# Shorter, more numerous unread products at the start, and the first local scores moved one step forward

## The chip, the cores and the metric

The kernel runs on one core of a Trainium2 chip. The metric is the device time of one execution in microseconds. Five runs of the kernel before the change gave 306.91, 307.11, 307.74, 307.89 and 309.62 us; the median is 307.74. The profile was taken of the run of 307.89 us. Its span, from the first to the last recorded work, is 306.1 us, so 1.8 us of the run lie around the span.

In this text PE is TensorE, DVE is VectorE, ACT is ScalarE, POOL is GpSimd and SP is SyncE. "PE weight load" is the instruction that puts the stationary operand in place ahead of a matmul.

## The reference

Attention with a sparse mask on 8 batches of 8 heads, 576 positions and 64 columns, followed by a two-layer MLP on the 4,608 tokens with a Mish activation:

```
pos = np.arange(S); rel = pos[:, None] - pos[None, :]
mask_local   = (rel >= 0) & (rel < 32)                                   # heads 0 to 3
mask_strided = (rel >= 0) & (pos[None, :] % 32 == pos[:, None] % 32)     # heads 4 to 7
scores = np.where(mask, q @ k.T / sqrt(64), -1e9)
attn   = softmax(scores)
x      = (attn @ v) as [tokens, 512]
h      = x @ w_in                       # 512 -> 2048
out    = (h * tanh(softplus(h))) @ w_out   # 2048 -> 512
```

## The kernel before

The attention of one batch is cut so that only the blocks that the masks leave are computed. A local head (kind "l") has 6 windows of 96 queries against 128 keys. A strided head (kind "s") is taken apart by position modulo 8: for each of 8 residues, 72 queries meet 72 keys. `PARTS` groups the score blocks of a batch into three parts for each kind, one accumulator (two PSUM banks, `acc(i)`, i from 0 to 2) for each part. So `("l", 0)` is the first local part: five (window, head pair) units, with two matmuls of 96 columns for each.

For batch 0 the mask is not multiplied in later. It is put under the scores: `Attn.bias` writes a large negative bias with two matmuls of a unit matrix against a constant (line 297), and `Attn.qk` adds the scores to it in the same accumulator (line 324), then lets ACT take the exponential (line 338). `Attn.pv2` multiplies two blocks of probabilities with v (lines 366 and 371: for strided blocks of batch 0 the values and the row sums come from two matmuls, of 64 columns and of one column), and DVE divides by the row sums (lines 396 and 397), which also frees the accumulator. `t_step` and `t_step_loc0` transpose q and k on PE (lines 237 and 253); DVE or ACT copies the result out of PSUM (lines 179 and 181). `xt` transposes the attention output for the MLP (lines 410 and 420).

The whole program is one order written out by hand (`manual_schedule`): the instructions stand on each engine in the order in which the Python code issues them, and semaphores make one engine wait for another. No planner moves them. Before the loop over the token blocks, batch 0 goes through alone. In order: memsets on DVE and the first loads; the unread products (`fill`, line 547: matmuls of a zeroed tile whose result nobody reads); transposes of strided k and q, with biases and more unread products between them; strided scores; then pairs of strided products `pv2("s", 0)`, `("s", 2)`, `("s", 4)`, `("s", 6)`, with the transposes of local k and q between the first three; local biases and scores; `xt` for the strided half; two unread products; the last local bias and scores; the local products `pv2("l", ...)`. Then begins the first block of the MLP (line 575 is the first layer, line 599 the second), and from there the loop runs 9 blocks of 512 tokens, with the attention of later batches placed between the matmul groups.

The accumulators in this stretch: pair ("s", 0) uses accumulator 0, pair ("s", 2) uses 1, pair ("s", 4) uses 2, pair ("s", 6) uses 0 again, local part 0 uses 1, local part 1 uses 2 and local part 2 uses 0.

Of the kernel before, what the change touches and what calls it, by code (L numbers as in the profile page):

```python
# [40 lines left out]
def kernel(ctx, tc, q, k, v, moe_w_in, moe_w_out, out):  # L41
# [34 lines left out]
    kTs = [const.tile([128, 16 * SU + 48], BF16, name=f"kTs{i}") for i in range(2)]  # L76
# [13 lines left out]
    def acc(i, name):  # L90

        return ps_a.tile([128, 2, 512], F32, tag=f"acc{i}", name=name)

    def tile_t(name):
        return ps_t.tile([128, 512], F32, tag="pt", name=name)
# [81 lines left out]
    def cast(eng, out_, in_):  # L177
        if eng is nc.scalar:
            nc.scalar.copy(out_, in_)  # L179
        else:  # L180
            eng.tensor_copy(out_, in_)  # L181
# [66 lines left out]
    def t_step_loc0(src, dst, hp, eng):  # L248

        tr = tile_t("tr")[:].bitcast(BF16)  # L250
        for j in range(CL):
            for e in range(2):
                nc.tensor.transpose(  # L253
                    tr[64 * e:64 * e + 64, PL * j:PL * j + PL], src[0:PL, 2 * hp + e, j, :],
                    ident[0:PL, 0:PL],
                )
        cast(
            eng, dst.rearrange("c (p j) -> c p j", j=CL),
            tr[:, 0:S].rearrange("c (j p) -> c p j", j=CL),
        )  # L260
# [280 lines left out]
        ]  # L541


    def fill(t, n):

        for _ in range(n):
            nc.tensor.matmul(
                t[:, 0:512], lhsT=kTs[1][:, 512:640], rhs=kTs[1][:, 0:512], start=True, stop=True
            )

    def fill_acc(i, n):
        fill(acc(i, "fill")[:, 0, :], n)

    def segs(t):
        a, e, o, r = 512 * t, 512 * t + 512, 0, []
# [80 lines left out]
    with tc.manual_schedule():  # L636
# [38 lines left out]
        cast(Dv, ks[0][0:PN, 0:2, :], k32[0:PN])  # L675

        a = Attn(0)
        fill_acc(2, 11)
        for hp in range(2):
            t_step(0, "k", hp, Sc if hp else Dv)  # L680
        a.bias("s", 0, 0)
        fill_acc(2, 3)
        for hp in range(2):
            t_step(0, "q", hp, Sc if hp else Dv)
        a.bias("s", 1, 1)
        fill_acc(2, 1)
        a.bias("s", 2, 2)
        for i in range(3):
            a.qk([("s", i)], i)
        fill(tile_t("fill"), 2)  # L690
        a.pv2("s", 0, 0)
        t_step_loc0(kl0, kTl[:, 0, 32:32 + S], 0, Sc)
        t_step_loc0(kl0, kTl[:, 1, 32:32 + S], 1, Sc)
        a.pv2("s", 2, 1)
        t_step_loc0(ql0, qTl[:, 0, :], 0, Sc)
        t_step_loc0(ql0, qTl[:, 1, :], 1, Sc)
        a.pv2("s", 4, 2)
        a.pv2("s", 6, 0)
        for i in range(2):
            a.bias("l", i, i + 1)  # L700
            a.qk([("l", i)], i + 1)
        for hp in range(2):
            rows_v_loc01(0, hp, Dv)
        load_v_loc_h(1)
# [126 lines left out]
```

## Time and profile before

| What | Value |
|---|---|
| median of 5 runs | 307.74 us (306.91 to 309.62) |
| the profiled run, and its span | 307.89 us, 306.1 us |
| PE busy | 298.6 us, 98% of the span |
| DVE, ACT, POOL busy | 155.2, 181.7, 105.2 us |
| mean granted clock of PE | 0.994 of full |
| first unread product (line 547) starts | 1.26 us |
| first strided product (line 366) starts | 10.58 us |
| first local bias (line 297, 480 columns) starts | 14.46 us |
| first local product (line 366, 65 columns) starts | 19.12 us |
| first MLP product (line 575) starts | 20.67 us |

The span is counted from its own start, and the times of the table are on that clock. Busy time of PE includes the depth of its pipeline, so matmuls overlap in it; the distance from one start to the next is the better measure of what a matmul takes. The granted clock is the share of full speed at which PE was allowed to run. A wait is shown behind the instruction that waited, with the instruction that released it. The wait names are inferred: where an instruction waits for several others, the one that came last is shown.

### The profile page before, as it was taken

To read this page: it belongs to the slowest core of one execution; us is meant where nothing else is said; L and a number is where in the kernel's file an instruction comes from. 1 tells how busy PE (TensorE), PEld (TensorE's weight loads), DVE (VectorE), ACT (ScalarE), POOL (GpSimd) and SP (SyncE) were. 2 spreads that over 40 slices of the span, in tenths; PEclk is the share of its full clock that TensorE was granted. 3 is DMA by queue.
4 is the path that set the end of the run, shared out by engine and by line. 5 is a ranking of instruction groups with operands and counts; after the bars stand their busy time and mean duration, and the time that the engine had idled before them with its cause. 6 is when DMAs were issued, how large, how long until landed. Compare 5 with 4: busy or idle time off the path is not lost.

```text
span 306.1 us, 5961 instructions
## 1 busy us (share of the span) xinstructions
PE 298.6 (98%) x2471; PEld 156.5 (51%) x2471; DVE 155.2 (51%) x375; ACT 181.7 (59%) x193; POOL 105.2 (34%) x119
## 2 busy tenths in 40 slices
PE   7999999999999999999999999999999999999995
PEld 3655555544554455444579654445444544444444
DVE  4463266301850077479877888787879850000000
ACT  2666635667446764767866786687668746216501
POOL 8752339860480246004950288029600000000000
PEclk9989999999999999999999999999999999999999
DMA  8999999999999999999759996896730120011011
GB/s 135 171 204 202 198 174 138 148 172 247 166 205 175 199 185 188 109 208 192 111 134 169 192 164 160 184 188 113 111 105 2 42 95 2 0 69 69 2 68 69
DMA packets 97550, 41.81 MB, mean 137 GB/s; under 512 B 79604, under 2 KB 91460, under 8 KB 97524
## 3 DMA queue, kind: packets, MB, share of 16 engines
q1 hardware_dynamic: 71708, 28.84, 52.4%
q0 software_dynamic: 25504, 12.31, 34.0%
q8 instruction: 19, 0.31, 0.5%
q10 hardware_dynamic: 312, 0.28, 0.3%
q14 instruction: 7, 0.06, 0.1%
HBM read 36.82 MB, written 9.44 MB: 151 GB/s over the span
## 4 chain that ended last, share of the span: by engine, by line
PE 91%; DVE 3%; DMA 2%; POOL 1%; issue 1%; ACT 1%; ACTq 0%; POOLq 0%
PE psh L575 41%; PE pso L599 34%; PE pso L626 5%; PE po L366 5%; PE ps L324 4%; DMA lq<-in_q_dram 2%; DVE x_l L383 1%; PE trx L410 1%; DVE x_s L383 1%; PE ps L297 1%; PE tr L253 1%; PE trx L420 1%; DVE rden L382 1%; ACT Ps L338 0%; DVE Pl L346 0%
## 5 line engine op out<-in xcount | busy, mean ns | idle before, releaser
L575 PE MATMUL psh<-xT,w_in 128*128 128x512 bf16 (+3 forms) x648 | 130.6, 355 | 0.7 <-DVE rden L396 0.5
L599 PE MATMUL pso<-w_out,gT 128*128 128x512 bf16 x512 | 121.7, 379 | 0.0
L581 ACT ACTIVATE gT<-psh 128x1024 bf16<-128x1024 f32 x72 | 72.5, 1024 | 46.1 <-PE psh L575 46.1
L575 PEld LDWEIGHTS <-w_in 128*128 128x128 bf16 x648 | 60.8, 98 | 55.3 <-issue 1.1
L599 PEld LDWEIGHTS <-gT 128*128 128x128 bf16 x512 | 45.4, 98 | 46.1
L445 DVE STREAM_TRANSPOSE xs_t<-x_s 32x512 bf16<-32x512 bf16 x48 | 33.7, 702 | 0.9
L606 ACT COPY osb<-pso 128x1024 f32<-128x1024 f32 x16 | 17.6, 1099 | 24.8 <-PE pso L599 14.4
L181 POOL CAST kl<-kl 96x768 bf16<-96x768 f32 x10 | 8.0, 822 | 69.7 <-DMA kl<-in_k_dram 69.7
L382 DVE RECIPROCAL rden<-po 72x4 f32<-72x4 f32 (+1 forms) x98 | 17.3, 177 | 28.7 <-PE po L366 28.5
L436 DVE STREAM_TRANSPOSE xT<-x_l 32x384 bf16<-32x384 bf16 x48 | 27.3, 569 | 0.7
L181 DVE COPY osb<-pso 128x512 f32<-128x512 f32 (+1 forms) x2 | 1.1, 558 | 51.3 <-PE pso L626 51.3
L346 DVE TENSOR_TENSOR Ps<-Ps,consts_sb 72x864 bf16<-72x864 bf16 (+3 forms) x12 | 6.6, 551 | 40.0 <-ACT Ps L338 40.0
L383 DVE TENSOR_TENSOR x_s<-po,rden 72x256 bf16<-72x256 f32 x56 | 23.5, 420 | 1.9
L338 ACT ACTIVATE Ps<-ps 72x864 bf16<-72x864 f32 (+3 forms) x21 | 17.4, 861 | 11.1 <-PE ps L324 11.0
L366 PEld LDWEIGHTS <-Ps 72*128 72x128 bf16 x256 | 15.6, 97 | 11.6 <-DVE Ps L346 0.8
L452 ACT COPY xT<-xs_t 128x576 bf16<-128x576 bf16 x8 | 21.4, 2937 | 0.0
L338 ACT ACTIVATE Pl<-ps 128x960 bf16<-128x960 f32 (+1 forms) x20 | 17.3, 876 | 4.0 <-PE ps L324 4.0
L383 DVE TENSOR_TENSOR x_l<-po,rden 96x256 bf16<-96x256 f32 x42 | 17.7, 421 | 1.4
L366 PE MATMUL po<-vs,Ps 72*128 72x65 bf16 (+1 forms) x256 | 18.2, 194 | 0.1
L179 ACT COPY xT<-trx 128x576 bf16<-128x576 bf16 x15 | 9.6, 639 | 13.0 <-PE trx L420 9.2
L181 POOL CAST vl<-vl 128x768 bf16<-128x768 f32 (+2 forms) x20 | 15.5, 774 | 3.2 <-PE po L366 2.0
L346 POOL TENSOR_TENSOR Ps<-Ps,consts_sb 72x1008 bf16<-72x1008 bf16 (+1 forms) x9 | 14.5, 1639 | 0.8 <-DVE x_l L383 0.7
(93 smaller groups left out, 239.7 us busy)
## 6 DMA issues: line engine op xcount, KB each, us to landing
out_dram<-osb SPq DMA_DIRECT2D x16, 512.0 KB, 4.0
kl<-in_k_dram SPq DMA_DIRECT2D x5, 576.0 KB, 7.2
ql<-in_q_dram SPq DMA_DIRECT2D x5, 576.0 KB, 11.6
vs<-in_v_dram SPq DMA_DIRECT2D x5, 576.0 KB
vl<-in_v_dram SPq DMA_DIRECT2D x5, 576.0 KB, 9.1
w_out<-in_moe_w_out_dram POOLq DMA_DIRECT2D x4, 512.0 KB, 16.6
ks<-in_k_dram POOLq DMA_DIRECT2D x7, 288.0 KB, 8.3
qs<-in_q_dram POOLq DMA_DIRECT2D x7, 288.0 KB, 8.1
```

Source lines behind the costliest of these rows:

```text
L181: eng.tensor_copy(out_, in_)
L338: nc.scalar.activation(pt[0:n, :, 0:nw], t[0:n, :, o0:o0 + nw], AF.Exp, scale=scale)
L346: meng.tensor_tensor(out=pm, in0=pm, in1=mk[0:n, :].unsqueeze(1).unsqueeze(1).to_broadcast([n, 2, nu, w]), op=ALU.mult,)
L366: nc.tensor.matmul(po[:, h, 0:rhs.shape[-1]], lhsT=pt[0:n, c0:c0 + 128], rhs=rhs, start=True, stop=True,)
L382: nc.vector.reciprocal(rden[0:m, :], po[0:m, :, D])
L383: nc.vector.tensor_tensor(out=dst.rearrange("p (h d) -> p h d", h=4), in0=po[0:m, :, 0:D], in1=rden[0:m, :].unsqueeze(2).to_broadcast([m, ...
L436: nc.vector.transpose(dst[32 * q:32 * q + 32, :, :, m:m + 32], src[m:m + 32, :, :, q, :])
L445: nc.vector.transpose(xs_t[32 * q:32 * q + 32, :, :, m:m + 32], src[m:m + 32, :, :, q, :])
L452: nc.scalar.copy(xT[:, 2 + c, t0:t0 + S].rearrange("p (n j) -> p j n", j=CS), xs_t[:, :, c, 0:PN])
L575: nc.tensor.matmul(ps[:, u, o:o + n], lhsT=w_in[:, cc, fc * 128:(fc + 1) * 128], rhs=xT[:, cc, a:a + n], start=(cc == 2 and o == 0), stop= ...
L581: nc.scalar.activation(gT[:, 2 * g:2 * g + 2, :], ps[:], AF.Mish)
L599: nc.tensor.matmul(p[:, ot % 2, :], lhsT=gT[:, fc, 128 * ot:128 * ot + 128], rhs=w_out[:, fc, :], start=(fc == 0), stop=(fc == 15),)
```

## The change

Two edits. The 11 unread products of 512 columns ahead of the strided transposes become 44 of 128 columns; the three other places with unread products keep 512. And the local part 0 moves forward: its bias is issued before the pair ("s", 4), and its scores between the pairs ("s", 4) and ("s", 6). The accumulators stay the same. On DVE, ACT, POOL and SP the order of instructions is not altered.

```diff
-    def fill(t, n):
+    def fill(t, n, w=512):
         for _ in range(n):
             nc.tensor.matmul(
-                t[:, 0:512], lhsT=kTs[1][:, 512:640], rhs=kTs[1][:, 0:512], start=True, stop=True
+                t[:, 0:w], lhsT=kTs[1][:, 512:640], rhs=kTs[1][:, 0:w], start=True, stop=True
             )
-    def fill_acc(i, n):
-        fill(acc(i, "fill")[:, 0, :], n)
+    def fill_acc(i, n, w=512):
+        fill(acc(i, "fill")[:, 0, :], n, w)
...
-        fill_acc(2, 11)
+        fill_acc(2, 44, 128)
...
         t_step_loc0(ql0, qTl[:, 1, :], 1, Sc)
+        a.bias("l", 0, 1)
         a.pv2("s", 4, 2)
+        a.qk([("l", 0)], 1)
         a.pv2("s", 6, 0)
-        for i in range(2):
-            a.bias("l", i, i + 1)
-            a.qk([("l", i)], i + 1)
+        a.bias("l", 1, 2)
+        a.qk([("l", 1)], 2)
```

## The prediction

> **What bounds the kernel now.** I read the page first. The busy shares say that TensorE (PE) sets the time, so a change pays only where it shortens PE's row or a wait in it.
>
> ```profile
> PE 298.6 (98%) x2471; PEld 156.5 (51%) x2471; DVE 155.2 (51%) x375; ACT 181.7 (59%) x193; POOL 105.2 (34%) x119
> PEclk9989999999999999999999999999999999999999
> ```
>
> Only 7.5 us of the 306.1 us span are idle on PE. The clock row has one slice below 9, the third (15.3 to 23.0 us), which the change touches. So I asked second for busy time and granted clock in equal stretches of the first 21 us, laid on the steps that the clock takes (columns: stretch, its length, busy us and instructions of PE, PE weight loads, VectorE, ScalarE and GpSimd, then granted clock, DMA share, GB/s).
>
> ```profile
> 0.71:4.12 3.41, 2.86 (x7) 1.03 (x8) 2.13 (x17) 1.28 (x1) 2.77 (x5) 1.00 0.64 135
> 4.12:7.53 3.41, 2.67 (x26) 1.22 (x24) 1.15 (x2) 0.64 (x1) 3.41 (x5) 1.00 1.15 161
> 7.53:10.95 3.42, 3.24 (x70) 2.00 (x70) 0.46 (x1) 1.96 (x3) 2.23 (x4) 1.00 1.23 180
> 10.95:14.36 3.41, 2.90 (x102) 2.58 (x100) 1.98 (x5) 3.04 (x6) 2.57 (x5) 1.00 2.00 170
> 14.36:17.77 3.41, 3.41 (x41) 1.56 (x38) 2.22 (x6) 1.55 (x3) 2.88 (x5) 0.50 1.55 183
> ```
>
> From 14.36 to 17.77 us PE is busy throughout at half clock. The first local scores, which the change moves, stand in that stretch. (The first row's 1.00 isn't what the fills show: up to 3.8 us they start 0.427 us apart, from 4.18 on 0.215.) Third, PE in order of time (start, length, source line, form, count):
>
> ```profile
> 1.26 3.94 PE L547 MATMUL fill<-kTs 128*128 128x512 bf16 x11 [1.26 <-DVE kTs L651]
> 5.95 0.69 PE L237 MATMUL tr<-consts_sb,ks 72*128 72x72 bf16 x16 [0.74 <-DVE ks L181]
> ...
> 12.90 0.70 PE L253 MATMUL tr<-consts_sb,lq 96*64 96x96 bf16 x24 [0.26 <-DMA lq<-in_q_dram]
> ...
> 14.46 0.96 PE L297 MATMUL ps<-consts_sb 128*128 128x480 bf16 x2
> 15.35 0.58 PE L324 MATMUL ps<-qTl,kTl 64*128 64x96 bf16 x10
> 15.87 0.98 PE L297 MATMUL ps<-consts_sb 128*128 128x480 bf16 x2
> 16.78 0.58 PE L324 MATMUL ps<-qTl,kTl 64*128 64x96 bf16 x10
> 17.29 0.90 PE L420 MATMUL trx<-consts_sb,x_s 72*128 72x72 bf16 x16
> 18.02 0.60 PE L547 MATMUL fill<-kTs 128*128 128x512 bf16 x2
> ```
>
> The fills end at 5.20 us and PE then stands 0.74 us until the cast of k is done. At 12.90 PE waits for the local q to land; from there to 20.19 it has no wait for another engine longer than 0.15 us. After 20.67 us the whole PE row follows, so what is gained or lost before that moves the end one for one. This holds while no load becomes late: the slices of w_in land at 17.0, 18.3, 21.6, 24.0 and 26.8 us (issue plus time to landing); the third is first needed near 24.7, so an earlier start has some 3 us of cover.
>
> **Part 1: 44 fills of 128 columns for 11 of 512.** The columns are the same, 5,632; 33 weight loads and 33 matmuls are added. The trace has no 128-column matmul. At full clock the nearest row is the 72-column transposes, 0.0325 us from start to start (72/2400 us plus 0.0025), at half clock 0.060 (72/1200). In both a weight load per product is hidden. By that row a 128-column fill takes 0.0558 us at full clock and 0.1067 at half. Up to 4.12 us, 26 fit into 2.86 us; the other 18 take 1.00; they end near 5.1 us, as now. [...] At half clock throughout they would take 44 x 0.1067 = 4.69 us and end at 5.95. k's cast releases PE at 5.9 by each, so the sum has 0 for this part. [...]
>
> What the fills do for the clock could matter more. [...] In the first window 2.86 us of 3.41 are columns flowing, 84%, whether in pieces of 512 or 128. I let the clock rise at 4.12 us as before: 0.
>
> **Part 2: the order of PE.** Now: pair (s,4), pair (s,6), bias l0, scores l0, bias l1, scores l1. Then: bias l0, (s,4), scores l0, (s,6), bias l1, scores l1. No instruction is added, and none moves on SP, POOL, VectorE or ScalarE; no DMA issue moves. New waits on PE:
> - Bias l0 writes the accumulator of pair (s,2), which VectorE is still reading: its multiply (L397) runs 12.92 to 13.61. With 0.1 us to release and load weights, bias l0 starts near 13.70; PE would have begun (s,4) at 13.53. Cost 0.17 us. All of PE is queued behind it, and VectorE's divisions wait for PE.
> - Scores l0 need both copies of local q on ScalarE, which end at 13.38 + 1.18 = 14.56. Bias l0 is 2 x 0.2025 = 0.405 us at full clock, to 14.11; pair (s,4), 0.435 at full clock, runs 14.14 to 14.36 and then at half rate to about 14.68. The copies are done: 0.
> - Bias l1 writes the accumulator of (s,4), read by VectorE from 14.88 to about 15.81. PE reaches it near 15.97: 0.
>
> The half-clock stretch swaps its contents. Bias l0 goes out: it cost 0.80 there (480/1200 each) and costs 0.405 now: -0.40. Half of (s,4) and all of (s,6), 12 of 16 couples of a 64-column and a 1-column product, come in. A couple takes 0.0545 us now; the last one before 14.46, partly in the slow stretch, took 0.082, and I take 0.080: 12 x 0.0255 = +0.30. One change of operand kind more: between bias and scores the slow stretch shows 0.14 beyond the columns, between pairs and bias 0.03; I take 0.10 (0.03 to 0.14). Sum 0.17 - 0.40 + 0.30 + 0.10 = +0.17. The transposes (L420) then start at 17.46 rather than 17.29, and fewer of their 16 fall into the slow stretch (5 for 8: -0.08). So fills start about **0.1 us** later (-0.1 to +0.3). The earlier exponential of l0 buys nothing: its reader, the first local product at 19.12, waits for PE's own order, and ScalarE had finished l1's too, at 18.37. Span 306.1 + 0.1 = 306.2; the profiled run 307.89 becomes 308.0. It was 0.15 above the median of 307.74, so the median becomes **307.8 us**.
>
> **Rivals.**
> 1. *The clock stays full from 14.36 on.* Between 10.95 and 14.36 PE is busy, but with narrow work: 26 couples of 65 columns are 0.70 us of flowing columns, 21%; the windows before have about 56% without transposes. [...] Then PE would run (s,4) to 14.6, scores l0 at 14.7, (s,6) to 15.4, wait 0.4 for VectorE's division of (s,4) to clear bias l1 at 15.8, and reach the transposes at 16.65, the first local product at 18.1 and the first MLP product near 19.7 in place of 20.67: -0.95, 306.8 us. It cannot give much more, as VectorE and ScalarE then end last.
> 2. *The gate opens late in the beginning* (the slower side). [...] One window: work that took 5.95 to 7.53 ends 0.8 us later, and PE's waits for loads before 12.90 (0.25 + 0.26 us) take up 0.5 of it: 308.1. Two windows: another 1.7 us, 309.8. It becomes slower by over 0.5% only where the gate is still shut at about 10 us. Against it: the 0.060 us starts at half clock, where weight loads leave no hole.
> 3. *The new wait decides.* In executions whose windows fall so that the gate doesn't close here, today's order has no wait at bias l1, and the changed one loses there 0.4 us and 0.2 at bias l0: 308.4.
> 4. *Nothing is to be seen*: both parts cost under 0.1 us: 307.7.
>
> **How the numbers follow.** The likeliest, at 0.5, is the sum, 307.8 (own range 307.3 to 308.4); rival 4 shares it at 0.1. Rival 1 has 0.14 (306.2 to 307.2), rival 3 has 0.1, rival 2 has 0.16, half of it beyond 309. A measurement of this kernel can tell about 0.5% (1.5 us) from no change: faster means below 306.2, slower above 309.3. The runs of before alone spread from 306.91 to 309.62. Faster: 0.11, from rival 1 with a window more in its favour. Slower: 0.17, from rival 2 and the tail of rival 3. Same: 0.72. The range takes in rivals 1, 3 and most of 2: 306.4 to 309.4.
>
> **What would show it.** Right: fills 0.107 us apart up to about 4.1 us and under 0.085 after, the k transposes still at 5.95 behind VectorE's cast; bias l0 waiting on VectorE near 13.6; a clock of 0.50 for 3.41 us after 14.4; the first local product within 0.3 us of 19.12. Wrong: a clock of 1.00 in that stretch (rival 1), starts 0.060 us apart in the k and q transposes (rival 2), or a second stretch at 0.50. [...] the borders may lie elsewhere in another execution; a shift of them would move the changed kernel and the one before alike, by up to 1.5 us.

## The result

The changed kernel takes 310.89 us (median of 43 runs, 307.49 to 315.06), the kernel before 307.9 (80 runs, 306.23 to 312.36). The ratio is 1.0068, 95% interval 1.0051 to 1.0085: slower by 2.1 us. The ratio leaves out executions more than 1.5% above the fastest of the same kernel (7 of the 43 of the changed one, all with a mean granted clock of 0.989 or less); the two medians, over all executions, lie 3.0 us apart. The prediction was 307.8 us with a range up to 309.4, and "same" at 0.72.

The profile that came with this result shows little of it, because its execution is one of the fastest: 307.95 us, span 306.2 us. Here are its busy shares, clock and transfers of program code, the same lines of the page as in the prediction; the last one reads the same in the page of the kernel before. Below them comes the stretch of PE around the moved scores, from the timeline.

```profile
PE 298.7 (98%) x2504; PEld 159.9 (52%) x2504; DVE 156.7 (51%) x375; ACT 181.5 (59%) x193; POOL 105.0 (34%) x119
PEclk9999999999999999999999999999999999999999
q8 instruction: 19, 0.31, 0.5%
```

```profile
1.27 4.87 PE L547 MATMUL fill<-kTs 128*128 128x128 bf16 x44 [1.27 <-DVE kTs L651]
5.93 0.95 PE L237 MATMUL tr<-consts_sb,ks 72*128 72x72 bf16 x16
...
13.95 0.58 PE L297 MATMUL ps<-consts_sb 128*128 128x480 bf16 x2
14.88 0.26 PE L324 MATMUL ps<-qTl,kTl 64*128 64x96 bf16 x4
15.69 0.30 PE L324 MATMUL ps<-qTl,kTl 64*128 64x96 bf16 x6 [0.56 <-issue]
```

The k transposes start where the prediction put them. The fills don't end there: all 44 start 0.107 us apart, at half clock (at full clock such fills start 0.056 us apart in the fills-only trace below), and end just ahead of the transposes, where the prediction's sum had 18 of them at full clock and an end near 5.1. New is the last line: in the middle of the ten score products of l0, PE stands still for 0.56 us, and the releaser is "issue": the profile shows no engine and no load that was waited for. Nothing like it is in the profile before.

A second profile of the changed kernel (with the last experiments below) has an execution of the usual kind, 311.47 us, span 309.7. Its timeline around the same place:

```profile
12.85 0.70 PE L253 MATMUL tr<-consts_sb,lq 96*64 96x96 bf16 x24 [0.23 <-DMA lq<-in_q_dram]
13.64 0.58 PE L297 MATMUL ps<-consts_sb 128*128 128x480 bf16 x2
14.56 0.26 PE L324 MATMUL ps<-qTl,kTl 64*128 64x96 bf16 x4
16.55 0.34 PE L324 MATMUL ps<-qTl,kTl 64*128 64x96 bf16 x6 [1.72 <-issue]
17.48 0.96 PE L297 MATMUL ps<-consts_sb 128*128 128x480 bf16 x2
...
23.36 0.86 PE L575 MATMUL psh<-xT,w_in 128*128 128x512 bf16 x3 [0.23 <-DVE rden L396]
```

And its stretches, laid on the steps of its clock (columns as in the prediction). In this text a window is a stretch of 3.41 us laid on such steps. The profile before has steps at 4.12, 14.36 and 17.77 us, 10.24 (3 x 3.413) and 3.41 us apart; the half-clock stretches are one window long there, two here, three in the traces of the fills alone and of the 33 one-column products. "The gate is closed" says no more than that the granted clock is 0.50 or, at the very beginning, where the clock reads 1.00, that products start as far apart as at half clock (0.427 us for 512 columns, up to 3.8 us in the profile before).

```profile
9.85:13.26 3.41, 2.98 (x91) 2.17 (x85) 1.46 (x4) 3.21 (x5) 2.34 (x4) 1.00 1.77 169
13.26:16.68 3.42, 1.62 (x42) 1.14 (x36) 1.21 (x3) 1.18 (x2) 2.84 (x5) 1.00 1.79 167
16.68:20.09 3.41, 3.41 (x51) 2.25 (x48) 2.02 (x5) 1.97 (x3) 2.23 (x3) 0.50 1.26 206
20.09:23.51 3.42, 3.13 (x33) 1.86 (x32) 1.41 (x5) 2.38 (x3) 0.69 (x1) 0.50 1.25 208
23.51:26.92 3.41, 3.41 (x31) 2.26 (x30) 2.86 (x5) 1.29 (x3) 0.73 (x2) 1.00 1.29 198
```

The hole is 1.72 us here. The window that holds it, 13.26 to 16.68, has 1.62 us of busy PE out of 3.42, and the two windows after it run at half clock. The first MLP product starts at 23.36 us for 20.67 in the profile before: 2.7 of the 3.6 us by which the span is longer. Some 0.8 us of the rest are two waits for the strided mask on VectorE later on.

The granted clock of each execution tells the same for all. One window at half clock lowers the mean by 3.41 x 0.5 / 306 = 0.0056, so 0.994 is one closed window, 0.989 two. (The half clock at the very beginning isn't in this number: the first profile has a mean of 1.000.) Median times by closed windows:

| | none | one | two | three and more |
|---|---|---|---|---|
| kernel before, 145 executions | 103: 307.63 us | 36: 309.00 | 4: 310.56 | 2: 311.92 |
| changed kernel, 67 executions | 17: 307.99 us | 14: 310.18 | 31: 311.13 | 5: over 312 |

With the clock open throughout, the changed kernel is 0.4 us slower. The larger part of the loss is that the gate closes in three of four executions in place of three of ten, and mostly for two windows.

### The profile page after: what moved, and what is told of

It reads as the page before. It is cut to its first block, busy times and chain, and to the rows that moved or that the text cites. A ratio compares the mean times of both kernels' runs of the same rounds, so it can differ in the third digit from the quotient of the medians.

```text
span 306.2 us, 6027 instructions
## 1 busy us (share of the span) xinstructions
PE 298.7 (98%) x2504; PEld 159.9 (52%) x2504; DVE 156.7 (51%) x375; ACT 181.5 (59%) x193; POOL 105.0 (34%) x119
## 4 chain that ended last, share of the span: by engine, by line
PE 90%; DVE 3%; ACT 2%; DMA 2%; issue 2%; POOL 0%; ACTq 0%; POOLq 0%
PE psh L575 41%; PE pso L599 33%; PE pso L626 5%; PE po L366 5%; PE ps L324 3%; DMA qs<-in_q_dram 2%; ACT Ps L338 1%; DVE x_l L383 1%; PE trx L410 1%; DVE x_s L383 1%; PE ps L297 1%; PE trx L420 1%; DVE rden L382 1%; PE tr L237 1%; PE tr L253 1%
## 5 line engine op out<-in xcount | busy, mean ns | idle before, releaser
L181 POOL CAST kl<-kl 96x768 bf16<-96x768 f32 x10 | 8.8, 904 | 65.8 <-DMA kl<-in_k_dram 56.2
```

## The experiments

All ratios are against the kernel before, on the same chip in the same batch, with a 95% interval. The theories are named in the expectations as they stood when each was written: A lays the cost on the short fills themselves, B on the new order, C on the 66 added instructions, as code that PE has to wait for.

### One part alone

The 44 short fills with the old order:

```diff
-        fill_acc(2, 11)
+        fill_acc(2, 44, 128)
```

> Only the 44 unread products of 128 columns; the order of biases, pairs and scores is that of the kernel before. Theory A [...]: this alone is slower by 0.6 to 0.8%, about 310 us, with a mean granted clock near 0.989 (two closed windows) in most runs. Theory B (the new order is what costs): within 0.2% of the kernel before. Theory C (66 more PE instructions shift the instruction fetch and PE stands still for code once): slower by 0.1 to 0.3%, with one hole of about 0.5 us on PE named issue, clock as before.

Measured: 311.31 us, ratio 1.0106 (1.0068 to 1.0144). The gate closed in all 6 executions. The wait of PE named issue up to 26 us, then its line of the timeline:

```profile
PE po L366 <- issue: 1.1, 1, 1.1
```

```profile
15.50 0.21 PE L366 MATMUL po<-vs,Ps 72*128 72x64 bf16 x1 [1.11 <-issue]
```

So the fills alone cost no less than both edits together (1.0066 beside them, below; the intervals overlap), and the hole is there again, but in front of another instruction: a strided product. In this trace the hole isn't what closed the gate first. The hole lasts from 14.39 to 15.50, but the half clock begins at 14.25, behind a window without a hole:

```profile
10.84:14.25 3.41, 3.19 (x102) 2.92 (x103) 1.78 (x4) 3.41 (x6) 2.42 (x5) 1.00 2.09 162
14.25:17.66 3.41, 2.30 (x29) 1.08 (x26) 2.38 (x6) 0.37 (x2) 2.91 (x4) 0.50 1.39 196
```

The first of these windows holds the same narrow work (102 products) as the one ahead of the closed window in the profile before, which has no hole either. What differs is that the clock then stays halved for three windows, to 24.49 (the mean clock of this execution is 0.983), for one before.

The new order with the 11 long fills:

```diff
+        a.bias("l", 0, 1)
         a.pv2("s", 4, 2)
+        a.qk([("l", 0)], 1)
         a.pv2("s", 6, 0)
-        for i in range(2):
-            a.bias("l", i, i + 1)
-            a.qk([("l", i)], i + 1)
+        a.bias("l", 1, 2)
+        a.qk([("l", 1)], 2)
```

> Only the new order; 11 unread products of 512 columns as before. Theory A: within 0.2% of the kernel before. Theory B (bias l0 waits for VectorE, later pairs come out later, PE's holes grow and the gate closes more often): slower by 0.6 to 0.8%, about 310 us, with a granted clock below that of the kernel before. Theory C: within 0.2%, and no hole named issue in the scores of l0.

Measured: 307.57 us, ratio 0.9993 (0.9976 to 1.0010). The gate stayed open in 20 of 22 executions. There is a hole of 0.31 us named issue, now at the last score product of l1:

```profile
13.57 0.58 PE L297 MATMUL ps<-consts_sb 128*128 128x480 bf16 x2
14.50 0.39 PE L324 MATMUL ps<-qTl,kTl 64*128 64x96 bf16 x10
15.59 0.58 PE L297 MATMUL ps<-consts_sb 128*128 128x480 bf16 x2 [0.18 <-DVE x_s L397]
16.10 0.38 PE L324 MATMUL ps<-qTl,kTl 64*128 64x96 bf16 x9
16.80 0.20 PE L324 MATMUL ps<-qTl,kTl 64*128 64x96 bf16 x1 [0.31 <-issue]
```

Theory B falls: the order costs nothing measurable. Theory C's expectation, no hole in the scores of l0, came true, but it had not foreseen the hole at l1.

The same count of instructions without short fills of 128 columns: 33 products of one column behind the 11 of 512, old order.

```diff
         fill_acc(2, 11)
+        fill_acc(2, 33, 1)
```

> The kernel before with 33 unread products of one column behind the 11 of 512: as many instructions as the changed kernel has, but hardly any columns and no 128-column product, old order. Theory A and B: within 0.2% of the kernel before (33 x 0.03 us end before the cast of k releases PE). Theory C: slower by 0.1 to 0.3% as in the fills-only kernel, with a hole on PE named issue between 12 and 20 us.

Measured: 312.76 us, ratio 1.0147 (1.0107 to 1.0186), the gate closed in all 6 executions. The hole is 1.96 us long:

```profile
PE po L366 <- issue: 2.0, 1, 2.0
```

The changed kernel beside them:

> The changed kernel beside the others on the same chip: ratio near 1.007, mean granted clock of most runs near 0.989; the kernel before should show 0.994 to 1.000 in most. Theory A expects its ratio to equal that of the fills-only kernel, theory B that of the order-only kernel; if both parts cost, it is about their sum.

Measured: 310.49 us, ratio 1.0066 (1.0043 to 1.0090), as in the result.

This points to the cause of the hole. The kernel with 33 one-column products has hardly a column more than the kernel before (33 on 5,632) and loses most. The width of the fills isn't what costs (theory A; the kernel below that keeps the 44 short fills and takes out other instructions says the same of their weight loads); 66 more PE instructions are. Theory C foresaw the hole but not the cost: it had 0.1 to 0.3%, the hole's own length. And in these traces the hole stands before the same ordinal, the 223rd matmul of PE, whatever that matmul is: a score product of l0 in the changed kernel, of l1 in the order-only one, a strided product in the two others. The page's line of code transfers suggests what is there: 19 transfers of 16 KB in the whole execution. I take them as PE's code: the page before counts 4,942 PE instructions (2,471 matmuls and as many weight loads) and 375 or fewer on any other engine. That makes some 260 in each, an estimate; a block, from here on, is what one such transfer brings. PE runs while they arrive (the first one is under way from 12.85 to 14.07 us in the profile before). In these traces the holes are 0.3 to 2.0 us long.

From the start times of PE's matmuls and of the code packets in the traces:

| kernel | first code transfer, us | ready for the 223rd, us | it starts | hole |
|---|---|---|---|---|
| before | 12.85 to 14.07 | 17.08 | 17.08 | none |
| order only | 13.62 to 15.40 | 16.28 | 16.80 | 0.31 |
| changed, first profile | 12.81 to 13.97 | 14.93 | 15.69 | 0.56 |
| changed, beside the experiments | 13.03 to 14.31 | 15.29 | 15.78 | 0.29 |
| changed, second profile | 13.53 to 15.13 | 14.62 | 16.55 | 1.72 |
| fills only | 12.76 to 13.99 | 14.22 | 15.50 | 1.11 |
| 33 one-column products | 13.33 to 15.04 | 14.32 | 16.45 | 1.96 |

("Ready" is the start of the matmul before it.) Where there is a hole, the matmul starts 1.4 to 1.7 us after the code transfer has ended, early or late (1.3 to 1.8 over all ten traces with a hole there). In the kernel before it was not needed sooner than 17.08, since PE ran at half clock from 14.36 on. The order-only kernel, whose gate stayed open, came a little too early.

### More and less of it, and the same instructions elsewhere

16 one-column products in place of 33:

```diff
         fill_acc(2, 11)
+        fill_acc(2, 16, 1)
```

> The kernel before with 16 (not 33) unread one-column products behind the 11 of 512; old order. Theory C now reads: PE's code comes in pieces, the piece that begins with the 223rd matmul is fetched while PE runs and is there only at 15.5 to 16.8 us, so a PE that gets there earlier stands still, and the hole then lets the clock gate close for two or three windows. With 33 the 223rd matmul is reached at 14.5, in the kernel before at 16.8. With 16 it is reached near 15.5: a hole of 0 to 1 us, ratio between 1.002 and 1.010. Theory D (it is not the place of the code but the thin work of one-column products itself that spoils the start): ratio about half of 1.0147, with no hole at the 223rd matmul.

Measured: 311.16 us, ratio 1.0062 (1.0035 to 1.0089); the gate closed in 15 of 22 executions. The medians over all executions, 311.16 and 307.85, lie 1.1% apart, so about half the instructions cost four tenths (by the ratios) to seven tenths (by the medians, 1.6% for 33) of what 33 did. In its trace the gate stays open and the hole is 0.42 us (the 222nd recorded matmul; some records are missing), so theory D's "no hole" is wrong.

33 one-column products behind the local products, ahead of the first MLP product:

```diff
         a.pv2("l", 4, 0)
+        fill(tile_t("fill"), 33, 1)
```

> The kernel before with the 33 one-column products not at the start but behind the local products, right before the first MLP product, where PE waits 0.47 us anyway; same count of instructions as the changed kernel, but the 223rd matmul stays where it was. 33 x 0.03 us less the 0.47 wait is about 0.5 us on the path: theory C expects a ratio of 1.000 to 1.003 and no hole. A theory that the mere number of instructions, wherever they stand, costs 1% or more expects 1.010 or more.

Measured: 307.54 us, ratio 0.9986 (0.9958 to 1.0014); the gate closed in 5 of 14 executions, near the share of the kernel before. So it isn't the number of instructions in the program; it is how many stand ahead of that block. The trace still has a hole of 0.28 us there, which theory C had not expected: with the gate open, the old order runs into the edge too.

### The 44 fills with their instructions paid back

In batch 0's strided products, the 64-column product and the one-column row sum become one product of 128 columns, 64 of v and 64 ones. That takes 32 matmuls and 32 weight loads out ahead of the block's edge. The main part of the edit (the ones are written by one more memset on VectorE):

```diff
...
-                rhs, tail = vsd[0][:, v0:v0 + D], vl[0][0:PN, 1, 0, D:D + 1]
+                nc.tensor.matmul(
+                    po[:, h, :].rearrange("p (a d) -> p a d", a=2),
+                    lhsT=pt[0:n, c0:c0 + 128], rhs=vs1[:, n0:33:32 - n0, :],
+                    start=True, stop=True,
+                )
...
```

With the 44 short fills in the old order:

> The 44 unread products of 128 columns, old order, and in the strided products of batch 0 the 64-column product and the one-column product for the row sum are made one of 128 columns (64 of v, 64 of ones): 32 matmuls and 32 weight loads fewer ahead of the scores of l0, about the same time on PE (0.056 for 0.0545 us). So the 223rd matmul falls within one matmul of where it stood before. Theory C: no hole, ratio 0.995 to 1.003. Theory A [...]: still slower by 0.8 to 1.1%, as the fills-only kernel.

Measured: 307.48 us, ratio 0.9980 (0.9959 to 1.0001), hole 0.35 us, the gate open in all 14 executions.

With the new order and 11 long fills:

> The new order with 11 unread products of 512, and the merged strided products as in the kernel with 44: 64 PE instructions fewer than before, so the code piece begins about 32 matmuls later. Theory C: the hole of 0.31 us that the order-only kernel had at the 223rd matmul is gone, clock 1.000 in nearly all runs, ratio 0.995 to 0.999; it would beat both kernels. If the order itself costs (new wait at bias l0), it stays at 0.999 to 1.001.

Measured: 307.51 us, ratio 0.9989 (0.9972 to 1.0006), no hole at the edge of the block, the gate open in all 22 executions.

With both edits of the change:

> The changed kernel, both edits, with the merged strided products (32 matmuls and 32 weight loads fewer ahead of the scores of l0), so that the 223rd matmul stands within one matmul of its place before. Theory C: no hole over 0.4 us there, clock 1.000 in nearly all executions, ratio 0.998 to 1.000 in place of 1.007. If the two edits cost by themselves: 1.005 or more.

Measured: 307.54 us, ratio 0.9986 (0.9969 to 1.0004); no hole, the gate open in all 22 executions. Its stretch around the scores of l0, where the changed kernel has 1.62 us of busy PE:

```profile
13.26:16.68 3.42, 3.36 (x65) 2.23 (x60) 2.15 (x6) 2.32 (x4) 2.48 (x4) 1.00 1.75 177
16.68:20.09 3.41, 2.89 (x48) 1.86 (x45) 2.69 (x7) 3.10 (x4) 2.61 (x4) 1.00 1.26 209
```

The whole change, with 44 short fills, costs nothing once as many instructions are taken out ahead of the edge. One caution: the merged products are other work than the pairs (128 columns in the time of 65, 0.056 us from start to start for 0.0545), and whether that has a part in the open gate isn't known. What they show of the hole is clean, what they show of the gate is not; there the one-column products ahead and behind carry the argument. None of the three is shown to beat the kernel before, since each interval includes 1. Their spread is smaller: the slowest of 22 executions of the merged kernel with the new order took 308.54 us.

### A hole without missing code, and an attempt on the transfer

ScalarE makes a useless copy between its two copies of local q, so that PE waits for it at the scores of l0. PE's instructions are untouched.

```diff
         t_step_loc0(ql0, qTl[:, 0, :], 0, Sc)
+        Sc.copy(vl32[:].rearrange("p h w d -> p (h w d)")[:, 0:1328], kTs[1][:])
```

> The kernel before, with no PE instruction added or moved; ScalarE makes one copy of zeros (128 x 1328, about 1.4 us) between its two copies of local q, so PE waits some 0.4 to 1.3 us at the scores of l0, near the place of the hole in the fills-only kernel. If a hole there, whatever makes it, lets the gate close over two or three windows: ratio 1.005 to 1.011, mean clock near 0.989 in most executions. If only the missing code costs and a hole is worth its own length: ratio 1.001 to 1.003, clock as in the kernel before.

Measured: 308.89 us, ratio 1.0031 (1.0008 to 1.0054); the gate closed in 11 of 22 executions. The waits of PE and the stretches of its profiled execution:

```profile
PE ps L324 <- ACT qTl L179: 0.4, 1, 0.4
```

```profile
12.89:16.30 3.41, 2.88 (x76) 2.19 (x75) 2.41 (x7) 3.41 (x5) 2.57 (x4) 1.00 1.82 168
16.30:19.71 3.41, 3.36 (x38) 2.01 (x38) 2.06 (x4) 2.26 (x4) 2.63 (x4) 0.50 1.28 206
19.71:23.13 3.42, 3.13 (x34) 1.80 (x33) 1.45 (x4) 2.10 (x3) 0.69 (x1) 0.50 1.24 207
```

A wait of 0.4 us made in another way goes with longer half-clock stretches, as the code hole does: two windows or more in 9 of 22 executions, for 6 of 145 of the kernel before. That the gate closes at all in half of them, for 29%, could still be chance in 22. The ratio is below the 1.005 of the full expectation and at the top of the 1.001 to 1.003 that the hole's length alone gave, but the clock is not as in the kernel before, so neither came true as a whole; the hole here was at the short end of its range.

Does the code wait behind the small packets of local v? In the kernel with 33 one-column products, v's loads go behind the first two slices of w_in:

```diff
-        load_v_loc_h(0)
-        for f0, f1 in ((0, 256), (256, 512), (512, 1024), (1024, 1536), (1536, 2048)):
+        load_w_in(0, 256)
+        load_w_in(256, 512)
+        load_v_loc_h(0)
+        for f0, f1 in ((512, 1024), (1024, 1536), (1536, 2048)):
             load_w_in(f0, f1)
```

> The kernel with 33 one-column products at the start, and the loads of local v of batch 0 (288 KB in 128-byte packets, on the chip from about 11 to 13.5 us) issued behind the first two slices of w_in instead of ahead of them. If the code piece, fetched from 13.3 us in the kernel with 33 products, waits behind those packets, its fetch starts 1 us or more earlier and the hole at the 223rd matmul shrinks from 1.96 us to under 1. If the fetch starts when PE asks for it, or has its own turn, it stays at 12.8 to 13.6 us and the hole at 1 to 2 us; v of l0 then comes later and the time stays at 1.010 or above.

Measured: 312.09 us, ratio 1.0152 (1.0096 to 1.0208). Inconclusive on the question: in its profiled execution (316.02 us) the gate didn't open before 27.7 us (products of 512 columns start 0.427 us apart from 1.67 on, 0.414 at 24.2, and 0.215 from 27.69), so PE reached the edge only at 19.4, the code transfer began at 17.18 and the hole was 0.42 us. It does show that the transfer doesn't begin at a fixed time: at 17.18 us here, with a PE that is late, for 12.76 to 13.62 in the table above.

The second profile of the changed kernel, which the result section used:

> One more look at the changed kernel, for a trace of an execution whose clock gate closes (about half of its executions have a mean clock of 0.989). Theory C: a hole named issue at the 223rd matmul between 14.3 and 16 us; where the clock mean is 0.994 or less, a stretch at half clock that begins at 10 to 15 us and takes one, two or three times 3.41 us, over the hole. About 310 to 311 us then; with a full clock about 308.

Measured: 311.47 us, mean clock 0.989, hole 1.72 us; the half-clock stretch of two windows began at 16.68, somewhat later than expected, right behind the window of the hole.

## Why the prediction was wrong

**The step that failed** is the sum of part 1: "k's cast releases PE at 5.9 by each, so the sum has 0 for this part". Its pieces held: fills start 0.107 us apart at half clock and, in the fills-only trace, 0.056 at full clock, so the row was right (512 columns take 0.427 and 0.215 us in the profile before, some 1,200 and 2,400 columns a us). The k transposes start at 5.93. But "33 weight loads and 33 matmuls are added" was costed only as time on PE. Instructions are also code, which has to arrive, by my reading in the page's 19 transfers of 16 KB. The 66 bring the edge of a code block forward from the scores of l1 to the last strided pair or the scores of l0, and PE reaches it at 14.2 to 15.3 us, before the block is there. Measured alone, part 1 is +1.06%, 3.3 us, for my 0. In its trace the hole is 1.1 us of that, and three windows at half clock, for one before, go with the rest. The line that should have raised the question was on the page before: 19 transfers of 16 KB. Of the signs of being wrong that were named, the first profile shows two, a clock of 1.00 and starts 0.060 us apart in the k transposes, and the second profile the third, a second stretch at 0.50, from 16.68 to 23.51 us.

That the first profile, 307.95 us, agrees with the 308.0 worked out is luck. Its clock stepped up only at 6.51 us, for 4.12 in the profile before, and PE stood still for 0.56 us at the hole; no window was closed after that, where the profile before has one. That the clock would rise at 4.12 us again was my estimate from one profile; no run shows what sets it.

**Part 2** was forecast at +0.1 us (-0.1 to +0.3). Order alone measured -0.07%, -0.2 us (-0.7 to +0.3). Bias l0 started at 13.57, 0.13 earlier than worked out, and bias l1 waited 0.18 for VectorE where I had 0. Within the changed kernel the order may help (fills alone 1.0106, both 1.0066 to 1.0068), but the intervals overlap, so that isn't shown.

**Rival 1** (the clock stays full) is what the order alone does: 20 of 22 executions. It gave no gain against the median because I read one profiled execution as the kernel. That one had a closed window; 103 of 145 executions of the kernel before have none. A closing is worth 1.4 us there (309.00 against 307.63), for the 0.95 worked out, but the median had nothing to win back. The low weight of this rival was my estimate; no run shows what decides whether the gate closes.

**Rival 2** had the right side, but a late opening is not what costs. The gate opened between 4.0 and 6.5 us in the profiles of the kernel before, the changed one and the two parts: at 4.1 with the 44 short fills in the old order, and near 6.1 with 11 long ones in the kernel with ScalarE's copy, so in these traces the opening isn't tied to the short fills. What matters is how long it is closed later, around the hole: two windows or more in 36 of 67 executions of the changed kernel, in 6 of 145 of the kernel before.

**Rival 3** (0.6 us lost in executions with an open gate) is not seen: order-only with an open gate 307.52, before 307.63.

The caveat at the end of the prediction, that a shift of the clock's windows "would move the changed kernel and the one before alike", is wrong as well: the changed kernel's gate closes more often and for longer.

**What stays open.** Why the block arrives so late: in the kernels with a hole, the next code transfer starts 3.6 to 3.8 us after the 223rd matmul, takes 0.9 to 1.0 us, and the first one shows another 1.4 to 1.7 from its end to use. The first one doesn't follow the block before it by a fixed time. 4,942 instructions in 19 transfers are some 130 matmuls with their weight loads a block, so that block begins near the 95th matmul (an estimate: 223 less some 130); the first transfer starts 2.7 to 4.0 us after it, and the 223rd matmul 5.5 to 7.0 us after it, in the ten traces with a hole. PE went from the 95th to the 222nd matmul in 4.5 us with 33 one-column products. Whether data transfers stretch the lag wasn't settled. Also open is what closes the gate. With the fills alone it closed ahead of the hole, and in the kernel before it closes without one; in the second profile the second window stays at half clock although PE is busy for all of the first (3.41 of 3.41 us). The counts show that kernels with holes of about 0.4 us or more in their traces close more often and for longer; how a hole does that they don't.

## What to carry to other kernels

Count an added instruction as code too, most of all in a stretch of short matmuls where PE goes through a 16 KB block in a few microseconds (the 95th to the 222nd matmul in 4.5 us with 33 one-column products): find the code transfers on the page, and ask which instruction the next block begins with and when PE gets there. A hole named "issue", without an engine or load behind it, that stays at the same ordinal while the work around it is reordered, was missing code here, in holes of 0.3 to 2.0 us. And before a sum is built on one profiled execution, look at how the clock of other executions is spread: with a wait of 0.4 us on PE, the executions that ran two windows at half clock took 310.40 us, 2.7 more than the kernel before takes with an open gate.

## What the runs showed of the hardware that was not expected

- 16 unread one-column products cost 0.62% by the ratio. They are some 0.4 us of PE work (an estimate: 16 x 0.027, half of a couple's 0.0545) ahead of the k transposes, where PE stood for 0.74 us before; 33 of them behind the edge cost nothing measurable.
- Products of 128 columns in place of 64 plus one took the same time on PE (0.056 us from start to start, for 0.0545), and in 58 executions of the three kernels that have them the gate never closed, against 42 of 145 in the kernel before. Whether the merged products or the missing hole did it was not separated.
- In one execution of the kernel with v's loads moved, PE ran at half clock from the start to 27.7 us (products of 512 columns start 0.427 us apart, from 27.69 on 0.215).
